# A spectral mixer on one core: column 0 of the filtered blocks given to GpSimd, with a new order of the middle stage

## The chip, the cores and the metric

The kernel runs on one core of one Trainium2 chip. The core has a matrix engine (TensorE, in the profile PE, with its weight loads as PEld), a vector engine (VectorE, DVE), an activation engine (ScalarE, ACT), a general engine (GpSimd, POOL) and an engine that here only issues transfers (SyncE, SP). Each engine runs its own queue of instructions in order; queues wait for each other through semaphores. The metric is the device time of one execution in microseconds, as the median of several runs.

## The reference

For `x` of 2048 tokens by 512 channels:

```python
xn = layernorm(x)                                  # over the 512 channels
s  = irfft2(rfft2(xn) * (w_r + 1j * w_i))          # a filter in two dimensions
u  = gelu(einsum("bsd,sf->bdf", xn, w1) + b1)      # mixes the tokens, f = 1792
y  = einsum("bdf,fs->bds", u, w2) + b2
out = x + s * silu(transpose(y))
```

All inputs and outputs are float32. The two matrix products of the mixer are the bulk of the work. A float32 operand is kept as a large part (the value rounded to what TensorE multiplies at speed) and a small part (the remainder), and a product is made of three products of parts: large by large, large by small, small by large.

## The kernel before

The tokens are cut into 16 tiles `j` of 128 tokens. The program has three stages, followed by a short tail of stores.

*First stage* (0 to 98 us): for each tile the layernorm's moments on VectorE, the normalised tile as large and small part (`hh`, `hl`), the products with seven of the fourteen blocks of `w1` (`hidden_early`, L396), and the first transform of the tile for the filter (`first_transform`, L226), whose result VectorE and GpSimd fold into the array `ey`. Ahead of the first product, TensorE runs `WARM` products of zeros (L385) from the tile `wz`, which GpSimd sets to zero (L373). `hidden_early` issues the large and then the small part of the weight against `hh`, calls `between`, which is the transform of this tile, and then multiplies by `hl`. The statistics of a tile are made by `stats` (L185), `spreads` (L189 to L195) and `scales` (L199 to L206).

*Middle stage* (98 to 204 us): the products with the other seven blocks of `w1` (the stream `h`, with `L683`, `L684` for the large weight part, `L686`, `L692` for the small one, `w1l`), between which the filter is worked off. The filter comes in four groups `n` with two halves `h` each. For each (n, h): TensorE transforms along the channels and forward (L591, L605); ScalarE takes the result from the accumulator into a block `e` (`taken`); two transfers on SyncE's queue make `z`, a copy of `e` with neighbouring rows swapped (`swapped`); VectorE works out the filtered block `pq` from `e`, `z` and the weights `wa`, `wb` in ten instructions (`weighted`); and TensorE transforms `pq` back (`way_back`, L670), 64 small products for both halves of `n`.

The column 0 of a block holds signals whose weights differ from the other columns (a real transform packs two real values there). GpSimd works it out apart in three instructions on 128x4 elements (`columns_apart`, the stream `s`): `z` times `e1`, `e` times `e2`, and their sum into the small tile `s1`; VectorE's copy then sets it over column 0 of `pq`. VectorE's instructions that write `e` must wait until GpSimd has read column 0 of it. Two rows of group 0 are special too: VectorE clears them in `z`, and GpSimd and VectorE combine the weights of these rows in `load_weights` and `ends_too`.

The order of all engines' work in the middle stage is written out by hand. Each letter of `STEPS` takes the next instruction from a stream: `h` products, `u` the filter's TensorE units, `r` raw weight loads, `a` large parts on ScalarE, `o` small parts on VectorE, `d` small parts by an accumulating transfer on GpSimd's queue (w1l 18, 20, to 28: ScalarE writes the negative of the large part, the transfer adds the raw weight), `g` gelu, `i`, `b` copies on ScalarE, `e` taken, `x` swapped, `s` GpSimd's column 0, `w` weighted, `l`, `t` loads of filter weights and tables, `f`, `q`, `m` forms of `u` for the second product (ScalarE's large parts, VectorE's small parts, VectorE's four sums). As each engine works in order, this list sets what stands behind what on every queue. `pq` has one buffer for each half `h`, so a block's first write waits for the `way_back` of the group before.

*Third stage* (204 to 375 us): eight passes `p` of products with `w2` (L961 to L967), whose parts ScalarE and VectorE make (L781, L782), the filter's last two transforms for the two tiles `p` and `p + 8` (L876, L885), the gates (L916) and `finish` (L926 to L931): it multiplies by the gate and stores. Tiles below 15 are stored by an accumulating transfer on GpSimd's queue onto `out`, into which `x` was copied earlier; tile 15 has `x` added on VectorE and is stored by SyncE.

## Time and profile before

| | |
|---|---|
| median of 3 runs | 379.05 us (379.03 to 380.07) |
| profiled execution | 381.97 us, span 380.2 us, granted clock 1.00 |
| TensorE busy | 369.4 us, 97% of the span |
| VectorE busy | 328.9 us, 87% |
| ScalarE busy | 213.8 us, 56% |
| GpSimd busy | 104.1 us, 27% |
| middle stage, 98 to 204 us | TensorE 104.2, VectorE 99.9, ScalarE 62.5, GpSimd 45.9 us busy |

In the profile a row of a timeline has the start, the duration, the engine, the source line, the operation, output and inputs by the program's names, and behind them in brackets how long the engine was idle before and what ended that. A row of groups ends with busy time and mean duration in ns, and behind the last bar the idle time before these instructions and its releasers. L128 is the line of the helper that issues the middle stage's instructions. A row of waits has an engine, what it worked on, whom it waited for, the total in us, the number of times and the longest.

### The profile page before, as it was taken

Reading aid. Unit: us, or ns where it says so; the run is one execution under the profiler, and the core shown is the slowest. Engines: PE = TensorE matmul, PEld = TensorE weight load, DVE = VectorE, ACT = ScalarE, POOL = GpSimd, SP = SyncE. Lnnn points to the kernel's source line nnn. Section 1 sums busy time; section 2 is a strip of 40 time slices with the busy share of each in tenths; the row PEclk is TensorE's granted clock in tenths of the full one; section 3 lists DMA queues with packets and bytes.
Section 4 is the critical chain, followed back from the end, with each engine's and each line's share of the span. In section 5 each row is a group of like instructions: output and inputs, shape, how many; then the busy total and the mean of one; then the engine's idle time right before and its main releaser. Section 6 shows DMA issues by size and latency. Waiting matters only on the chain.

```text
span 380.2 us, 6865 instructions
## 1 busy us (share of the span) xinstructions
PE 369.4 (97%) x2417; PEld 311.8 (82%) x2417; DVE 328.9 (87%) x717; ACT 213.8 (56%) x391; POOL 104.1 (27%) x134
## 2 busy tenths in 40 slices
PE   8999999999999999999999999999999999999994
PEld 4888888888778676778688787798988888888994
DVE  6899999867799999999978895998888988898873
ACT  4677765754973365855466753564555455545641
POOL 2133233243420835856300021030302021110100
PEclk9999999999999999999999999999999999999999
DMA  7957468214546777999863898989989889895711
GB/s 252 344 166 225 151 203 256 81 42 140 145 160 201 240 230 267 260 279 314 182 177 52 234 249 184 269 161 265 192 222 198 204 212 183 229 195 180 99 22 41
DMA packets 42087, 73.28 MB, mean 193 GB/s; under 512 B 4196, under 2 KB 25444, under 8 KB 41924
## 3 DMA queue, kind: packets, MB, share of 16 engines
q1 hardware_dynamic: 35460, 58.88, 49.3%
q0 software_dynamic: 6592, 13.96, 22.2%
q8 instruction: 19, 0.31, 0.3%
q14 instruction: 16, 0.13, 0.1%
HBM read 60.24 MB, written 8.13 MB: 180 GB/s over the span
## 4 chain that ended last, share of the span: by engine, by line
PE 83%; DVE 9%; DMA 3%; issue 2%; ACT 2%; POOL 0%; DVEq 0%; ACTq 0%; POOLq 0%
PE ps L396 20%; PE ps L961 16%; PE ps L963 8%; PE ps L683 6%; PE ps L684 5%; PE ps L967 5%; PE ps L591 4%; PE ps L226 4%; PE ps L692 4%; PE ps L885 3%; PE ps L876 3%; DMA s<-in_w_dram 3%; DVE pq L128 2%; DVE e L128 2%; PE ps L670 1%
## 5 line engine op out<-in xcount | busy, mean ns | idle before, releaser
L396 PE MATMUL ps<-h,w1h 128*128 128x512 f32 x224 | 58.7, 398 | 0.0
L781 ACT ACTIVATE w2f<-s 128x896 fp32r<-128x896 f32 x32 | 30.2, 947 | 32.4 <-DVE s L808 16.9
L396 PEld LDWEIGHTS ps<-h,w1h 128*128 128x128 f32 x224 | 40.9, 188 | 7.9
L772 POOL DMA_DIRECT2D s<-in_w_dram x16 | 13.8, 864 | 118.1 <-DVE es L890 31.4
L782 DVE TENSOR_TENSOR w2f<-s,w2f 128x896 fp32r<-128x896 f32 x32 | 34.8, 1089 | 11.9 <-ACT w2f L781 11.3
L683 PE MATMUL ps<-h,w1h 128*128 128x512 f32 x112 | 45.0, 401 | 0.0
L684 PE MATMUL ps<-h,w1h 128*128 128x512 f32 x112 | 43.7, 390 | 0.0
L128 POOL TENSOR_TENSOR s<-z,e 128x4 f32<-128x4 f32 x8 | 27.4, 3429 | 37.3 <-DMA z<-e 25.2
L961 PE MATMUL ps<-fa,w2f 128*128 128x512 f32 x98 | 36.3, 406 | 0.4 <-DVE p L909 0.4
L961 PE MATMUL ps<-fc,w2f 128*128 128x512 f32 x98 | 35.2, 397 | 1.4 <-DVE p L909 0.9
L961 PE MATMUL ps<-fb,w2f 128*128 128x512 f32 x98 | 35.8, 402 | 0.0
L782 DVE TENSOR_TENSOR w2f<-a,w2f 128x896 fp32r<-128x896 f32 x24 | 26.1, 1087 | 6.1 <-ACT w2f L781 6.1
L396 PE MATMUL ps<-h,w1l 128*128 128x512 f32 x112 | 30.6, 389 | 0.0
L781 ACT ACTIVATE w2f<-a 128x896 fp32r<-128x896 f32 x24 | 22.6, 948 | 13.6 <-PE ps L963 9.3
L128 ACT ACTIVATE w1h<-w1s 128x512 fp32r<-128x512 f32 (+1 forms) x30 | 17.5, 582 | 22.6 <-PE ps L684 13.0
L683 PEld LDWEIGHTS ps<-h,w1h 128*128 128x128 f32 x112 | 21.0, 188 | 9.2 <-issue 5.0
L963 PE MATMUL ps<-fc,w2f 128*128 128x256 f32 x98 | 27.7, 283 | 0.4 <-DVE w2f L782 0.4
L963 PE MATMUL ps<-fa,w2f 128*128 128x256 f32 x98 | 27.7, 282 | 0.1
L963 PE MATMUL ps<-fb,w2f 128*128 128x256 f32 x98 | 27.6, 282 | 0.0
L928 POOL DMA_DIRECT2D out_dram<-g x16 | 14.2, 887 | 44.6 <-DVE g L926 44.6
L692 PE MATMUL ps<-h,w1l 128*128 128x512 f32 x93 | 25.6, 391 | 0.1
L396 PEld LDWEIGHTS ps<-h,w1l 128*128 128x128 f32 x112 | 21.0, 188 | 4.6
(179 smaller groups left out, 918.4 us busy)
## 6 DMA issues: line engine op xcount, KB each, us to landing
a<-in_w_dram SPq DMA_DIRECT2D x24, 448.0 KB
s<-in_w_dram POOLq DMA_DIRECT2D x17, 448.0 KB, 7.5
s<-in_w_dram SPq DMA_DIRECT2D x15, 448.0 KB
w1r<-in_w_dram SPq DMA_DIRECT2D x16, 256.0 KB
z<-e SPq DMA_DIRECT2D x16, 256.0 KB
w1s<-in_w_dram SPq DMA_DIRECT2D x16, 256.0 KB
yj<-ey SPq DMA_DIRECT2D x16, 256.0 KB
x<-in_x_dram SPq DMA_DIRECT2D x15, 256.0 KB
```

The lines of the kernel that those rows point to most:

```text
L128: return lambda *a, **k: keep(getattr(engine, name)(*a, **k))
L226: T.matmul(z[:, b], h[:, b * P:(b + 1) * P], c, start=True, stop=True)
L396: T.matmul(ps[:, bank + i], w[wi][:, i * P:(i + 1) * P], hj, start=first and j == 0, stop=last and j == NJ - 1)
L591: keep(T.matmul(pd[:, b * P:(b + 1) * P], ey[:, lo, b].rearrange("p h j -> p (h j)"), cd[:, b], start=True, stop=True))
L683: keep(T.matmul(o, wh[:, sl], hh[j], start=first, stop=False))
L684: keep(T.matmul(o, wh[:, sl], hl[j], start=False, stop=False))
L692: keep(T.matmul(ps[:, bank], wl[:, k * P:k * P + P], hh[j], start=False, stop=final))
L781: ordered(A.activation(wf[:, 0], v, AF.Copy))
L782: ordered(V.tensor_sub(wf[:, 1], v, wf[:, 0].bitcast(F32)))
L961: in_turn(j0, T.matmul(o, wf[:, 0, i], u, start=m == 0 and not joins, stop=end, skip_group_check=True))
L963: in_turn(j0, T.matmul(o[:, HD:], wf[:, 1, i], u[:, :HD], start=False, stop=end, skip_group_check=True))
L967: T.matmul(o, wf[:, wi, i], ui, start=m + a == 0 and opens, stop=end and a == 2, skip_group_check=joins)
```

## The change

- `WARM` goes from 16 to 12, and `wz` is a tile of 128 columns that the warm-up products read four times.
- In the first tile, `normed_v` comes before the shift `nb` (new function `shifts`); the small part of the first weight is made before the second tile's moments, and the second tile's `spreads` and `scales` come later. The transform of tile 0 comes behind its products with `hl`.
- Column 0 is GpSimd's from end to end: `columns_apart` writes the sum into column 0 of `pq` itself, `weighted` works on the columns from 1 on, and VectorE's copy is gone. The clearing of the special rows of `z` and the combination of their weights go to GpSimd.
- `STEPS` is another list.
- In `finish`, the right half of tile 7 has `x` added on VectorE (loaded as `x0`) and is stored by SyncE, as tile 15's halves are.

```diff
@@ -21,15 +21,15 @@
 NH = NF // 2
 FORMS = (2, 1, 0, 3, 4, 5, 6)
 NS = 25
-WARM = 16
+WARM = 12
 LATE = 16
 ADDED = range(NJ + 2, 2 * NJ - 2, 2)
 STEPS = (
-    "aahoguogogurigurfifrqufqirqhfmhiqmumahmfthoeerhfxmuxqaxmuxiomruqifmuiqhfwswhisswhgfwsfsuwsahwehwwhwl"
...
+    "orauaroghorghiugrguiffqufqihqfmiqhamumhoftmhreefxumaxqxuioxmruqimugmihfhswsihsfqfswfusqahswhshowrweh"
...
 )
 SPLIT = 4
 
@@ -195,12 +195,16 @@
                 keep(V.bn_aggr(m["mv"][:, i], m["st"][:, i]))
             roots(m)
 
-        def scales(m):
+        def shifts(m):
+            keep(V.scalar_tensor_tensor(m["nb"], m["mv"][:, :, 0:1], -1.0, m["rs"][:, :, 1:2], op0=ALU.mult, op1=ALU.mult))
+
+        def scales(m, alone=False):
             keep(V.reciprocal(m["r0"], m["sd"]))
             keep(V.tensor_mul(m["t"], m["r0"], m["r0"]))
             keep(V.scalar_tensor_tensor(m["t"], m["t"], -0.5, m["v2"], op0=ALU.mult, op1=ALU.mult))
             keep(V.scalar_tensor_tensor(m["rs"], m["t"], 1.5, m["r0"], op0=ALU.add, op1=ALU.mult))
-            keep(V.scalar_tensor_tensor(m["nb"], m["mv"][:, :, 0:1], -1.0, m["rs"][:, :, 1:2], op0=ALU.mult, op1=ALU.mult))
+            if not alone:
+                shifts(m)
 
             G.tensor_mul(m["q"], m["rs"][:, :, 0:1], m["rs"][:, :, 1:2])
             G.tensor_mul(m["q"], m["q"], m["v2"][:, :, 1:2])
@@ -369,7 +373,7 @@
             return t[:, k]
 
 
-        wz = lnp.tile([P, D], BF16, name="wz", tag="e")
+        wz = lnp.tile([P, P], BF16, name="wz", tag="e")
         G.memset(wz, 0.0)
         WA, WB = (0, 4, w1p, 4), (NH, 3, wbp, 3)
         xs[0] = lnp.tile([P, D], F32, name="x0", tag="x", bufs=5)
@@ -382,7 +386,7 @@
         SY.dma_start(cf, c_f)
         load_x(2)
         for _ in range(WARM):
-            T.matmul(ps[:, 0], wz[:, :P], wz, start=True, stop=True)
+            T.matmul(ps[:, 0].rearrange("p (b c) -> p b c", c=P), wz, wz.unsqueeze(1).to_broadcast([P, 4, P]), start=True, stop=True)
 
         def high(dst, src):
             keep(A.activation(dst, src, AF.Copy))
@@ -396,9 +400,9 @@
                     T.matmul(ps[:, bank + i], w[wi][:, i * P:(i + 1) * P], hj, start=first and j == 0, stop=last and j == NJ - 1)
             products(0, hh[j], True, False)
             products(1, hh[j], False, False)
-            r = between()
+            r = between() if j else None
             products(0, hl[j], False, True)
-            return r
+            return r or between()
 
         m = moments("m0", 2)
         for i, c_ in enumerate(halves):
@@ -409,18 +413,19 @@
         w = w1_tiles(0, *WA), w1_tiles(0, *WB)
         h = new_h(0)
         high(w[0][0], raws[0, 0])
-        scales(m)
+        scales(m, alone=True)
         normed_v(hh[0], xs[0], m, 0, 1)
+        shifts(m)
         normed(h, xs[0], m, 0)
         m1 = moments("m1", 1)
+        low(w[0][1], raws[0, 0], w[0][0])
         stats(m1, 0, xs[1])
-        low(w[0][1], raws[0, 0], w[0][0])
-        spreads(m1, 1)
         high(w[1][0], raws[0, 1])
         c = turned(0, m, 0)
         low(hl[0], h, hh[0])
+        spreads(m1, 1)
+        low(w[1][1], raws[0, 1], w[1][0])
         scales(m1)
-        low(w[1][1], raws[0, 1], w[1][0])
         of = {1: (m1, 0)}
         m = moments("m2", 2)
         of.update({2: (m, 0), 3: (m, 1)})
@@ -543,12 +548,10 @@
                 SY.dma_start(w[:2, 0], wx[:, 0:3:2])
                 SY.dma_start(w[2:], wk[2:, at:at + 2, i::2])
                 SY.dma_start(w[:2, 1], wk[:2, at + 1, i::2])
-                G.tensor_sub(w[:2, 0, 1 - i], w[:2, 0, 1 - i], w[:2, 0, i])
-
-        def ends_too(k, i):
-            if k == ends // 2:
-                one, two = (weights[k, i][:2, 0, a] for a in (1 - i, i))
-                V.scalar_tensor_tensor(two, two, 2.0, one, op0=ALU.mult, op1=ALU.add)
+                one, two = (w[:2, 0, a] for a in (1 - i, i))
+                G.tensor_sub(one, one, two)
+                G.tensor_add(two, two, two)
+                G.tensor_add(two, two, one)
 
         def place(n, h):
             places[n, h] = [mp.tile([P, 2, 2, 256], F32, name=f"{c}{n}_{h}", tag=f"ez{h}", bufs=2) for c in "ez"]
@@ -576,7 +579,7 @@
         G.tensor_copy(e2[:2, ends, 1:2], e1[:2, ends, 1:2])
         G.tensor_scalar(e1, e1, sg[:, 0:1], None, op0=ALU.mult)
 
-        hfs, s1s, back = {}, {}, {n: [] for n in range(4)}
+        hfs, back = {}, {n: [] for n in range(4)}
 
         def load_tables(n):
             if n not in gfs:
@@ -619,23 +622,30 @@
             yield SY.dma_start(z[0::2], e[1::2])
             yield SY.dma_start(z[1::2], e[0::2])
 
+        def products_of(n, h):
+
+            k = 2 * n + h
+            if k not in pqs:
+                pqs[k] = new_pq(n, h)
+            return pqs[k]
+
         def columns_apart(n, h):
 
             at, (e, z) = 4 * n + 2 * h, places[n, h]
-            s1 = s1s[n, h] = mp.tile([P, 2, 2, 2], F32, name=f"s1_{n}_{h}", tag="s1")
+            if at == ends:
+                yield G.memset(z[:2, 0], 0.0)
+            s1 = mp.tile([P, 2, 2, 2], F32, name=f"s1_{n}_{h}", tag="s1")
             yield G.tensor_mul(s1[:, 0], z[:, :, :, 0], e1[:, at:at + 2])
             yield G.tensor_mul(s1[:, 1], e[:, :, :, 0], e2[:, at:at + 2])
-            yield G.tensor_add(s1[:, 0], s1[:, 0], s1[:, 1])
+            yield G.tensor_add(products_of(n, h)[:, :, :, 0], s1[:, 0], s1[:, 1])
 
         def weighted(n):
 
             for h in range(2):
                 at, k = 4 * n + 2 * h, 2 * n + h
                 e, z = places[n, h]
-                if at == ends:
-                    yield V.memset(z[:2, 0], 0.0)
-                pq = pqs.pop(k, None) or new_pq(n, h)
-                er, ei, zr, zi, pr, pi = (a[:, :, s] for a in (e, z, pq) for s in range(2))
+                pq = products_of(n, h)
+                er, ei, zr, zi, pr, pi = (a[:, :, s, 1:] for a in (e, z, pq) for s in range(2))
                 V.scalar_tensor_tensor(pr, zi, sg[:, 0:1], er, op0=ALU.mult, op1=ALU.add)
                 yield
                 V.scalar_tensor_tensor(pi, zr, sg[:, 0:1], ei, op0=ALU.mult, op1=ALU.subtract)
@@ -644,12 +654,9 @@
                 yield
                 V.scalar_tensor_tensor(ei, zr, sg[:, 1:2], ei, op0=ALU.mult, op1=ALU.subtract)
                 yield
-                for i in range(2) if k == ends // 2 else ():
-                    yield ends_too(k, i)
-                V.tensor_mul(pq, pq, weights[k, 0])
-                yield
-                V.tensor_mul(e, e, weights[k, 1])
-                yield
+                for a, i in ((pq, 0), (e, 1)):
+                    V.tensor_mul(a[..., 1:], a[..., 1:], weights[k, i][..., 1:])
+                    yield
                 V.tensor_add(pr, pr, pi)
                 yield
                 V.tensor_add(er, er, ei)
@@ -657,8 +664,6 @@
                 V.tensor_sub(pi, pr, er)
                 yield
                 V.tensor_add(pr, pr, er)
-                yield
-                V.tensor_copy(pq[:, :, :, 0], s1s[n, h][:, 0])
                 back[n].append(pq)
                 yield
 
@@ -924,7 +929,7 @@
 
         def finish(g, j, cols, y, xr=None):
             V.tensor_mul(g[:, cols], y[:, cols], g[:, cols])
-            if j + 1 < NJ:
+            if xr is None:
                 G.dma_start(out[:, j, cols], g[:, cols], accum_op=ALU.add)
             else:
                 V.tensor_add(g[:, cols], g[:, cols], xr[:, cols])
@@ -942,6 +947,8 @@
             if p == NP - 1:
                 xr = fp.tile([P, D], F32, name="xr", tag="yj", bufs=3)
                 SY.dma_start(xr, x[:, NJ - 1])
+                x0 = w2p.tile([P, NH * P], F32, name="x0", tag="s1", bufs=1)[:, :D]
+                SY.dma_start(x0[:, right_], x[:, j0, right_])
             both = p + 1 < NP
             bx, by, bz, bw = (ps[:, b] if both else ps[:, b, :HD] for b in (2 + p % 2, 4, 5, 1))
             for k, n in enumerate(ORDER if p + 1 < NP else LAST):
@@ -985,7 +992,7 @@
                 elif n == 3:
                     gate(g0, j0, right_, summed(f"c12_{p}", bz, v2), 1.0)
                     if p:
-                        finish(g0, j0, whole if p + 1 < NP else right_, y0)
+                        finish(g0, j0, *((whole, y0) if p + 1 < NP else (right_, y0, x0)))
                     else:
                         y0 = channels(j0, yt0)
                         yt1 = sequence(j1, yb)
```

Line numbers after the change are 4 higher in the first stage and 5 higher from the middle stage on (L670 becomes L675, L692 becomes L697, L926 becomes L931).

VectorE's queue at the end of block (0,1), where its second half of the filter's first group is finished, before:

```order
L128 TENSOR_TENSOR pq0_1_1326<-pq0_1_1326,e0_1_1324 128x2x256 [waits DVE_49]
L128 TENSOR_TENSOR w1l_11_1645<-w1s11_1593,w1h_11_1644 128x384 [waits DMAHW4_49,DMAHW5_49,PE_49,Activation_49]
L128 COPY pq0_1_1326<-s1_0_1_1515 128x4 [waits DVE_49,Pool_49]
L128 TENSOR_TENSOR w1l_12_1666<-w1s12_1608,w1h_12_1665 128x384 [waits DMAHW0_49,DMAHW1_49,PE_49,Activation_49]
L128 TENSOR_TENSOR fb1_1481<-u1_1294,fb1_1481 128x2x256
L128 TENSOR_TENSOR fd0_1511<-u0_1358,fd0_1511 128x256
L128 TENSOR_TENSOR fa0_1512<-u0_1358,fa0_1512 128x2x256
```

and in the change:

```order
L128 TENSOR_TENSOR pq0_1_1326<-pq0_1_1326,e0_1_1324 128x2x255 [waits DVE_49]
L128 TENSOR_TENSOR w1l_11_1637<-w1s11_1582,w1h_11_1636 128x384 [waits DMAHW4_49,DMAHW5_49,PE_49,Activation_49]
L128 TENSOR_TENSOR w1l_12_1660<-w1s12_1595,w1h_12_1659 128x384 [waits DMAHW6_49,DMAHW7_49,PE_49,Activation_49]
L128 TENSOR_TENSOR fa0_1510<-u0_1374,fa0_1510 128x2x256
L128 SCALAR_TENSOR_TENSOR pq1_0_1718<-z1_0_1556,sg_1304,e1_0_1555 128x2x255 [waits DMAHW0_49,DMAHW1_49,PE_49,Pool_49]
```

The copy is gone, and the form subtractions `fb1` and `fd0`, which stood here, now stand ahead of block (0,1).

GpSimd's queue for the blocks (3,0) and (3,1), before:

```order
L128 TENSOR_TENSOR s1_3_0_2117<-s1_3_0_2117 128x4 [waits Pool_49]
L128 DMA w1l_24_2177<-in_w1_dram 128x2x256 [waits DMASW2_49,DMASW0_49,Activation_49]
L128 TENSOR_TENSOR s1_3_1_2228<-z3_1_2083,e1_69 128x4 [waits DMAHW3_49,DMAHW2_49,DVE_49]
L128 TENSOR_TENSOR s1_3_1_2228<-e3_1_2082,e2_70 128x4
L128 TENSOR_TENSOR s1_3_1_2228<-s1_3_1_2228 128x4 [waits Pool_49]
L128 DMA w1l_26_2235<-in_w1_dram 128x2x256 [waits DMASW3_49,DMASW1_49,Activation_49]
```

and in the change:

```order
L128 TENSOR_TENSOR pq3_0_2167<-s1_3_0_2103 128x4 [waits DVE_49,PE_49,Pool_49]
L128 DMA w1l_24_2176<-in_w1_dram 128x2x256 [waits DMASW2_49,DMASW0_49,Activation_49]
L128 TENSOR_TENSOR s1_3_1_2211<-z3_1_2065,e1_69 128x4 [waits DMAHW2_49,DMAHW1_49]
L128 TENSOR_TENSOR s1_3_1_2211<-e3_1_2064,e2_70 128x4
L128 TENSOR_TENSOR pq3_1_2224<-s1_3_1_2211 128x4 [waits DVE_49,Pool_49]
L128 DMA w1l_26_2231<-in_w1_dram 128x2x256 [waits DMASW3_49,DMASW1_49,Activation_49]
```

The sums now write `pq`, and that of (3,0) waits for TensorE, which must have read the `pq` of the group before; the transfers of `w1l` still stand behind them.

TensorE's queue at `way_back(3)`, before:

```order
L684 MATMUL ps_58<-h10_97,w1h_26_2234 128x512
L692 MATMUL ps_58<-h10_97,w1l_26_2235 128x512 [waits DMASW3_49,Activation_49]
L692 MATMUL ps_58<-h10_97,w1l_26_2235 128x512 x3
L670 MATMUL ps_58<-pq3_0_2188,hf3_1955 32x256 [waits DMAHW5_49,DVE_49]
L670 MATMUL ps_58<-pq3_0_2188,hf3_1955 32x256 x7
L670 MATMUL ps_58<-pq3_1_2265,hf3_1955 32x256 [waits DVE_49]
```

and in the change:

```order
L675 MATMUL ps_58<-pq3_0_2167,hf3_1949 32x256 [waits DMAHW5_49,DVE_49,Pool_49]
L675 MATMUL ps_58<-pq3_0_2167,hf3_1949 32x256 x7
L675 MATMUL ps_58<-pq3_1_2224,hf3_1949 32x256 [waits DVE_49,Pool_49]
L675 MATMUL ps_58<-pq3_1_2224,hf3_1949 32x256 x7
L675 MATMUL ps_58<-pq3_0_2167,hf3_1949 32x256 x8
L675 MATMUL ps_58<-pq3_1_2224,hf3_1949 32x256 x8
L688 MATMUL ps_58<-h10_97,w1h_26_2230 128x512
L689 MATMUL ps_58<-h10_97,w1h_26_2230 128x512
L697 MATMUL ps_58<-h10_97,w1l_26_2231 128x512 [waits DMASW3_49,Activation_49]
```

`way_back(3)` stands ahead of the second half of part 26 instead of behind it, and waits for GpSimd too.

8 lines of the change are left out of this document (4 added, 4 removed).

## The prediction

> **What bounds the kernel now.** I read the page's busy shares first, then the waits of TensorE, then the three places at which the change works: the start, the middle stage from 98 to 204 us, and the last few microseconds.
>
> ```profile
> PE 369.4 (97%) x2417; PEld 311.8 (82%) x2417; DVE 328.9 (87%) x717; ACT 213.8 (56%) x391; POOL 104.1 (27%) x134
> ...
> 98.00:204.00 106.00, 104.18 (x848) 81.02 (x848) 99.91 (x166) 62.48 (x109) 45.94 (x38) 1.00 0.77 222
> ...
> PE ps L670 <- DVE pq L128: 1.2, 2, 0.7
> PE ps L686 <- DVE w1l L128: 0.5, 1, 0.5
> ```
>
> TensorE is busy for 369.4 of 380.2 us, at a granted clock of 1.00 in the middle stage (second row: the stage, its length, then the busy time of TensorE's products, its weight loads, VectorE, ScalarE and GpSimd, with instruction counts), and no product is removed that the reference needs. So the change can win only what TensorE does not spend on products: its waits, the start before the first product and the end behind the last. In the middle stage VectorE is busy 99.91 of 106 us, nearly as full as TensorE (104.18), and it is VectorE that TensorE waits for there: for the filtered block `pq` and for the small part `w1l` of a weight. A microsecond taken off VectorE is worth something only up to these waits. The profiled execution took 381.97 us, its span of 380.2 and 1.8 around it; the median of the runs, 379.05 us, is 2.9 lower. I work out differences inside the profiled span, where what lies around it stays, and take them off the median.
>
> **The end: -0.7 us.**
>
> ```profile
> 374.47 0.86 POOL L928 DMA_DIRECT2D out_dram<-g  x1 [9.58 <-DVE g L926]
> 375.14 0.47 ACT L916 ACTIVATE g<-ps,b2t 128x256 f32<-128x256 f32 x1 [1.42 <-PE ps L967]
> 375.65 0.43 DVE L926 TENSOR_TENSOR g<-y,g 128x256 f32<-128x256 f32 x1 [1.47 <-ACT g L916]
> 376.11 0.42 DVE L930 TENSOR_TENSOR g<-g,xr 128x256 f32<-128x256 f32 x1
> ...
> L1042 POOLq DRAIN  x3: 46/93/4971, 374.4 to 379.9; - x3
> L1042 SPq DRAIN  x3: 7/7/7, 378.6 to 379.7; - x3
> ```
>
> GpSimd issues its last store at 374.47, and its drain, which begins there, takes 4.97 us: to 379.4. SyncE, which sends the really last result after 376.5, is through at 378.7. So GpSimd's drain is the last to arrive, by 0.7 us. The change makes that store a plain one on SyncE, with the addition of `x0` on VectorE; the drain then starts after GpSimd's store before it, some 9.6 us earlier by the idle time in the first row. The added 128x256 addition (0.42, as L930's) falls into the 1.47 us that VectorE idles before 375.65; without that cover it would cost its 0.42. The `x0` load, 128 KB more on SyncE's queue, has the whole last pass to land. Range 0 to -0.8.
>
> **The start: -0.2 us.**
>
> ```profile
> 0.75 0.52 POOL L373 MEMSET wz<- 128x512 bf16 x1
> 1.33 5.38 PE L385 MATMUL ps<-wz 128*128 128x512 bf16 x16 [1.33 <-POOL wz L373]
> 5.04 1.18 PEld L385 LDWEIGHTS <-wz 128*128 128x128 bf16 x6 [0.16 <-issue]
> ...
> 5.26 0.63 ACT L388 ACTIVATE w1h<-w1r 128x512 fp32r<-128x512 f32 x1 [0.78 <-DMA w1r<-in_w_dram]
> 5.37 0.54 DVE L212 TENSOR_SCALAR h<-x,mvm,rsm 128x512 fp32r<-128x512 f32 x1
> 6.36 1.27 PE L396 MATMUL ps<-h,w1h 128*128 128x512 f32 x4
> ```
>
> The operands of the first product are there at 5.37 + 0.54 = 5.91 and 5.26 + 0.63 = 5.89, but the sixteen warm-up products hold TensorE until 6.36. Their last six follow each other every 0.2 us (1.18 for six), so without four of them the warm-up ends 0.8 us earlier, at about 5.5, earlier still as the memset fills a quarter of the columns; the first product can come at 5.9, 0.45 earlier. Against it, the second tile's small statistics now stand behind one more subtraction of some 0.6 us on VectorE, and later tiles do not come 0.45 us earlier; I take 0.2. With the warm-up over before the products begin, a gap of some 0.4 us opens on TensorE; the trace has none of that kind to price, so it is bounded by nothing and by the whole gain. Range 0 to -0.6.
>
> [...]
>
> **The middle: -1.8 us.** Here VectorE loses work:
>
> ```profile
> L128 DVE COPY pq<-s 128x4 f32<-128x4 f32 x8 | 1.3, 163 | 0.1
> L128 DVE MEMSET z<- 2x512 f32 x1 | 0.5, 485 | 0.0
> L128 DVE SCALAR_TENSOR_TENSOR wa<-wa 2x256 f32<-2x256 f32 x1 | 0.4, 406 | 0.0
> L128 DVE SCALAR_TENSOR_TENSOR e<-z,sg,e 128x512 f32<-128x512 f32 x16 | 11.3, 745 | 0.3 <-POOL s L128 0.3
> ...
> L128 POOL TENSOR_TENSOR wb<-wb 2x256 f32<-2x256 f32 x1 | 0.8, 776 | 0.0
> ```
>
> Eight copies at 0.08 start to start (129.89 to 129.97 below) are 0.65; memset 0.5; the special-row instruction 0.41, less the 0.08 by which neighbours overlap, and its like for `wb`, 0.67; the waits for GpSimd's reading of column 0 0.3: together 2.1 us. Blocks of 255 columns in place of 256 save 0.4%, which I leave out. GpSimd gets the memset and four additions of 0.78 next to the one shown, 3 us, ahead of its 12.1 us of idleness before block (0,0) (the idle time in the row of its first products, under rival 1).
>
> ```profile
> 128.77 0.66 PE L670 MATMUL ps<-pq,hf 32*32 32x256 f32 x16
> 128.82 0.67 DVE L128 TENSOR_TENSOR pq<-pq,e 128x512 f32<-128x512 f32 x1
> 129.43 0.54 DVE L128 TENSOR_TENSOR w1l<-w1s,w1h 128x384 fp32r<-128x384 f32 x1
> 129.89 0.15 DVE L128 COPY pq<-s 128x4 f32<-128x4 f32 x1
> 129.97 0.54 DVE L128 TENSOR_TENSOR w1l<-w1s,w1h 128x384 fp32r<-128x384 f32 x1
> 130.10 1.36 PE L670 MATMUL ps<-pq,hf 32*32 32x256 f32 x48 [0.67 <-DVE pq L128]
> ...
> 147.14 0.54 DVE L128 TENSOR_TENSOR w1l<-w1s,w1h 128x384 fp32r<-128x384 f32 x1
> 150.00 1.60 PE L670 MATMUL ps<-pq,hf 32*32 32x256 f32 x64
> ...
> 187.82 0.66 PE L670 MATMUL ps<-pq,hf 32*32 32x256 f32 x16
> 188.98 1.36 PE L670 MATMUL ps<-pq,hf 32*32 32x256 f32 x48 [0.50 <-DVE pq L128]
> ```
>
> `way_back(1)` has its blocks in time and takes 1.60. `way_back(0)` takes 128.77 to 131.46, 1.1 too long, and `way_back(3)` 187.82 to 190.34, 0.9 too long; with 0.5 for `w1l` these are the 2.5 us to be had. (0) Ahead of block (0,1) VectorE loses memset, special rows, one copy and 0.1 of waits, 1.4 us, and takes on two form subtractions that stood behind it (0.6 start to start for 128x512, as from 128.82 to 129.43, and 0.33 for half of it): it is 0.45 earlier. Its last addition ends at 129.05, and TensorE no longer waits for the `w1l` and the copy behind it but goes on at about 129.1 in place of 130.10: 1.0 won. (1) At 147.14 VectorE is then 1.8 earlier (1.4, the rest of the waits, two copies) and TensorE 1.0: the 0.5 goes, 1.5 in all. (3) `way_back(3)` now stands 1.4 us earlier in TensorE's order, half a part of products, and VectorE's block comes 2.1 earlier; so TensorE, 1.5 earlier, still loses about 0.6 of the 0.9. Sum 1.0 + 0.5 + 0.3 = 1.8. The third stage is fed by loads whose room `way_back(3)` frees, so what is won there is not given back to the loads. Bounds: nothing where other waits take the place, -2.5 where all go.
>
> Sum: -0.7 - 0.2 - 1.8 = -2.7, **376.4 us**. The middle's 1.8 stands on GpSimd being in time: `way_back` on TensorE, with all products behind it, now waits for GpSimd's addition into `pq`, that addition waits for the `way_back` before, and the `w1l` transfers of GpSimd's queue stand behind it.
>
> **Rival 1, slower: GpSimd is locked out.**
>
> ```profile
> L128 POOL TENSOR_TENSOR s<-z,e 128x4 f32<-128x4 f32 x8 | 27.4, 3429 | 37.3 <-DMA z<-e 25.2 <-DVE z L128 12.1
> ...
> 124.96 8.47 POOL L128 TENSOR_TENSOR s<-z,e 128x4 f32<-128x4 f32 x1 [10.16 <-DMA z<-e]
> 133.39 0.20 POOL L128 TENSOR_TENSOR s<-e,e 128x4 f32<-128x4 f32 x1
> 135.53 0.72 POOL L128 TENSOR_TENSOR s<-z,e 128x4 f32<-128x4 f32 x1 [1.67 <-DMA z<-e]
> 175.81 4.15 POOL L128 TENSOR_TENSOR s<-z,e 128x4 f32<-128x4 f32 x1 [3.49 <-DMA z<-e]
> 181.29 1.20 POOL L128 DMA_DIRECT2D w1l<-in_w_dram  x1
> ...
> w1l<-in_w_dram POOLq DMA_DIRECT2D x6, 256.0 KB, 6.0
> ...
> 133.62 1.45 DVE L128 SCALAR_TENSOR_TENSOR e<-z,sg,e 128x512 f32<-128x512 f32 x2 [0.25 <-POOL s L128]
> 179.82 0.17 DVE L128 COPY pq<-s 128x4 f32<-128x4 f32 x1
> ```
>
> A product of 128x4 that takes 0.20 us undisturbed took 8.47 and 4.15. The long ones end where VectorE, busy until then with two-input instructions, idles for GpSimd (133.43, before 133.62) or runs a copy (179.96); the one at 135.53 got in at the next boundary, 0.72. The change takes away just these openings. The place is block (3,1): if its first product, ready at about 174, misses the boundaries, VectorE next pauses between dependent `u` subtractions behind the block, whose last addition I put 2.1 and some before `way_back(3)`'s 188.98: at about 185.6. Behind it 1.3 us (179.96 to 181.29) and 6.0 of transfer: `w1l` lands at about 193, where TensorE wants it behind `way_back(3)`, at 188.98 + 1.36 - 2.9 = 187.4. Cost 5.5, less the 2.7: 381.8. It decides from an entry later than about 180 (187.4 - 6.0 - 1.3) on. For it speaks the mean of 3.43 us of eight first products; against it, that some got in at once, and that VectorE will also pause for `w1l` buffers that TensorE still reads.
>
> [...]
>
> **Rival 2, no change: it costs only block (1,0).** If that one (ready at about 124.5) is held until the dependent `u` instructions (six instructions behind the `w1l` of 147.14, which comes at 145.3: at about 148), the six instructions of (1,0) and (1,1) follow at some 0.4 each; `way_back(1)`, due at 150.00 - 1.5 - 0.5 = 148.0 (it stands half a microsecond of products earlier too), waits 2.5 us: nearly all of the 2.7 is gone, 379.0. For it: 8.47 us at just this block.
>
> **Rival 3: only the ends pay.** Another wait takes the place of those in the middle, as ScalarE's for the buffers of blocks that GpSimd still reads. Then -0.9: 378.1.
>
> **How the numbers follow.** Forecast 0.50, rival 1 0.25, rival 2 0.15, rival 3 0.10. A difference within 0.3% (1.1 us) cannot be told from none. Faster: 0.50 and half of rival 3, 0.55; same: the rest of it and rival 2, 0.20; slower 0.25. The forecast's own range is 375.2 (all terms at the far bound: 3.9 off) to 377.9; the whole range, 375.0 to 381.9, takes in rivals 2 and 3 and half of rival 1, 0.85 in all.
>
> **What would show it.** Right: no idle before L675 for `way_back(0)` over 0.5, none for `w1l` by VectorE at 146, GpSimd's first products under 3 us or ended by 180, first product at 5.9, SyncE last at the end. Wrong: TensorE's waits name POOL or a `w1l` transfer at L675 or L697; a first product of `s` over 10 us; first products at L400 at twice their 0.2 us pace.

## The result: 376.38 us, a ratio of 0.992

The kernel with the change takes 376.38 us (median of 6 runs, 376.13 to 378.69), the kernel before beside it 379.32 (6 runs, 379.03 to 380.07). The ratio is 0.9918, with a 95% interval of 0.990 to 0.9937: faster, by more than the 0.3% that can be told from no change. On another chip a second comparison gave 0.9932 (0.9899 to 0.9965). The profiled execution took 378.69 us, its span 376.9, the granted clock 1.00. The ratios of this document leave out executions in which the chip was in a slower state, so they can differ by some 0.1% from the quotient of the medians beside them.

The page's row of busy times, and the windows view of the middle stage (its length, then busy time of TensorE's products, its weight loads, VectorE, ScalarE and GpSimd), of the changed kernel:

```profile
PE 368.5 (98%) x2413; PEld 311.1 (83%) x2413; DVE 326.8 (87%) x707; ACT 213.5 (57%) x391; POOL 107.4 (28%) x138
...
97.90:201.80 103.90, 103.48 (x849) 80.86 (x848) 97.29 (x154) 62.10 (x109) 50.45 (x44) 1.00 0.78 226
```

VectorE lost 2.6 us of work in the middle stage (97.29 for 99.91 before; 0.4 of it is one instruction on `u` that no longer falls into the stage), and the stage is 2.2 us shorter (103.9 for 106.1). TensorE is still what the stage is full of.

TensorE's waits in the changed kernel (L968 was L961 before: from the last pass's two new lines on, line numbers are 7 higher):

```profile
PE ps L890 <- ACT yt L883: 1.2, 1, 1.2
PE ps L389 <- POOL wz L377: 1.0, 1, 1.0
PE ps L968 <- DVE fc L300: 0.5, 1, 0.5
...
PE ps L675 <- DVE pq L128: 0.4, 2, 0.2
```

The wait for `w1l` is gone from this list, that for the filtered block `pq` has fallen from 1.2 to 0.4, and a new one, for `yt`, stands in the third stage; "start alone" below, with the old middle stage, has it too (0.6).

TensorE's timeline at the places of the prediction:

```profile
128.40 0.66 PE L675 MATMUL ps<-pq,hf 32*32 32x256 f32 x16
129.25 1.35 PE L675 MATMUL ps<-pq,hf 32*32 32x256 f32 x48 [0.19 <-DVE pq L128]
...
147.86 1.50 PE L675 MATMUL ps<-pq,hf 32*32 32x256 f32 x64
...
184.61 0.66 PE L675 MATMUL ps<-pq,hf 32*32 32x256 f32 x16
185.45 1.35 PE L675 MATMUL ps<-pq,hf 32*32 32x256 f32 x48 [0.18 <-DVE pq L128]
...
187.30 1.09 PE L697 MATMUL ps<-h,w1l 128*128 128x512 f32 x4
```

`way_back(0)` now takes 128.40 to 130.60, 2.2 us for 2.7 before, and `way_back(3)` 184.61 to 186.80, 2.2 for 2.5. An undisturbed one takes 1.50, as `way_back(1)` at 147.86.

Where the span went is best seen stage by stage. The table gives the start of the first product, the end of the first stage's last product, and from there the time to the first `w2f` product (middle), to the end of the last product (third), and to the end of the span, worked out from the start and end times of TensorE's rows in each trace. The experiments are explained below.

| kernel | first product | first stage ends | middle | third | behind last product |
|---|---|---|---|---|---|
| before | 6.36 | 97.91 | 106.1 | 171.1 | 5.1 |
| start alone | 5.95 | 97.72 | 106.2 | 168.9 | 5.1 |
| end alone | 7.07 | 98.43 | 106.1 | 168.0 | 4.2 |
| list alone | 6.89 | 98.25 | 106.5 | 168.1 | 5.0 |
| code alone | 6.17 | 97.97 | 103.2 | 173.8 | 5.2 |
| code and list | 6.98 | 98.34 | 103.8 | 168.0 | 5.1 |
| code and end | 7.43 | 98.79 | 103.2 | 171.0 | 4.2 |
| full change | 6.16 | 97.92 | 103.9 | 170.9 | 4.2 |
| full change, again | 6.04 | 97.80 | 103.9 | 169.1 | 4.2 |

Between the two profiled executions, then: start 0.0, middle -2.2, third stage -0.2, end -0.9, together -3.3. The columns "middle" and "behind last product" fall into two groups each, whatever else varies; the third stage varies between the traces by up to 5.7 us, with old and new code alike (see the last section). So the terms of the sum can be read stage by stage where the whole times scatter too much.

### The profile page after: what moved, and what is told of

It is laid out like the page before. It is cut to its first block, busy times and chain, and to the rows that moved or that the text cites. A ratio compares the mean times of both kernels' runs of the same rounds, so it can differ in the third digit from the quotient of the medians.

```text
span 376.9 us, 6860 instructions
## 1 busy us (share of the span) xinstructions
PE 368.5 (98%) x2413; PEld 311.1 (83%) x2413; DVE 326.8 (87%) x707; ACT 213.5 (57%) x391; POOL 107.4 (28%) x138
## 3 DMA queue, kind: packets, MB, share of 16 engines
HBM read 60.38 MB, written 8.13 MB: 182 GB/s over the span
## 4 chain that ended last, share of the span: by engine, by line
PE 78%; DVE 10%; DMA 6%; ACT 3%; issue 2%; SPq 0%; DVEq 0%; ACTq 0%
PE ps L400 18%; PE ps L968 15%; PE ps L970 8%; PE ps L688 6%; PE ps L689 6%; PE ps L974 5%; PE ps L697 4%; PE ps L594 4%; PE ps L230 3%; DMA a<-in_w_dram 3%; PE ps L890 3%; PE ps L881 3%; DMA s<-in_w_dram 2%; DVE pq L128 2%; PE ps L675 1%
## 5 line engine op out<-in xcount | busy, mean ns | idle before, releaser
L400 PEld LDWEIGHTS ps<-h,w1h 128*128 128x128 f32 x224 | 40.8, 188 | 9.0 <-ACT w1h L392 1.2
L786 ACT ACTIVATE w2f<-s 128x896 fp32r<-128x896 f32 x32 | 30.2, 947 | 29.9 <-DVE s L813 16.9
L968 PE MATMUL ps<-fa,w2f 128*128 128x512 f32 x98 | 36.3, 406 | 0.4 <-DVE p L914 0.4
L968 PE MATMUL ps<-fb,w2f 128*128 128x512 f32 x98 | 35.8, 402 | 0.0
L968 PE MATMUL ps<-fc,w2f 128*128 128x512 f32 x98 | 35.1, 397 | 0.5 <-DVE fc L300 0.5
L688 PEld LDWEIGHTS ps<-h,w1h 128*128 128x128 f32 x112 | 21.0, 188 | 8.9 <-issue 5.0
L697 PE MATMUL ps<-h,w1l 128*128 128x512 f32 x93 | 25.7, 391 | 0.0
L689 PEld LDWEIGHTS ps<-h,w1h 128*128 128x128 f32 x112 | 21.1, 188 | 3.9
```

Source lines behind the costliest of these rows:

```text
L400: T.matmul(ps[:, bank + i], w[wi][:, i * P:(i + 1) * P], hj, start=first and j == 0, stop=last and j == NJ - 1)
L688: keep(T.matmul(o, wh[:, sl], hh[j], start=first, stop=False))
L689: keep(T.matmul(o, wh[:, sl], hl[j], start=False, stop=False))
L697: keep(T.matmul(ps[:, bank], wl[:, k * P:k * P + P], hh[j], start=False, stop=final))
L786: ordered(A.activation(wf[:, 0], v, AF.Copy))
L968: in_turn(j0, T.matmul(o, wf[:, 0, i], u, start=m == 0 and not joins, stop=end, skip_group_check=True))
```

## The experiments

**The pieces one by one.** The first four runs put the change's pieces into the kernel before. "End alone" adds only the plain store:

```diff
-            if j + 1 < NJ:
+            if xr is None:
                 G.dma_start(out[:, j, cols], g[:, cols], accum_op=ALU.add)
...
+                x0 = w2p.tile([P, NH * P], F32, name="x0", tag="s1", bufs=1)[:, :D]
+                SY.dma_start(x0[:, right_], x[:, j0, right_])
```

> The kernel before with the plain store of tile 7's right half alone. Theory: GpSimd's drain is the last to arrive at the end, and the store moved to SyncE takes it off: 0.7 to 0.95 us less than before, all of it behind the last product. Rival: the end is bound by SyncE's own last store and its landing; then nothing, or 0.4 more by the addition on VectorE.

Measured: 379.05 beside 379.77, a ratio of 0.9993 (0.9961 to 1.0024). The times cannot tell 0.7 from nothing here. The traces can: 4.2 us behind the last product in this and in every other kernel that has the plain store, 5.0 to 5.2 in every one without. The end is worth 0.9.

"Start alone" is the full change with the middle and the end taken back: `WARM = 12`, the memset of a quarter of the columns, and the first tiles' small steps in their new order.

```diff
-WARM = 16
+WARM = 12
...
-        scales(m)
+        scales(m, alone=True)
         normed_v(hh[0], xs[0], m, 0, 1)
+        shifts(m)
```

> The kernel before with the change's start alone (12 warm-up products, the new order of the first tile). Theory after the two profiles: no gain, within 0.15 us of before, because the first product comes 0.2 us earlier but tile 2's transform starts where it did (19.95 before, 19.94 after). Rival, as predicted: 0.2 us less.

Measured: 379.79, ratio 1.0005 (0.9979 to 1.0032): no gain in the time that this comparison could show, though an interval of 1 us to either side does not exclude a few tenths.

"Code and list" is the columns' code on GpSimd with the new list `STEPS`, with the old start and end. Its diff is the middle part of the change, of which this is the core:

```diff
-    "aahoguogogurigurfifrqufqirqhfmhiqmumahmfthoeerhfxmuxqaxmuxiomruqifmuiqhfwswhisswhgfwsfsuwsahwehwwhwl"
+    "orauaroghorghiugrguiffqufqihqfmiqhamumhoftmhreefxumaxqxuioxmruqimugmihfhswsihsfqfswfusqahswhshowrweh"
...
-            yield G.tensor_add(s1[:, 0], s1[:, 0], s1[:, 1])
+            yield G.tensor_add(products_of(n, h)[:, :, :, 0], s1[:, 0], s1[:, 1])
...
```

> The kernel before with column 0 on GpSimd and the new list, with before's start and end. Theory: the third stage begins 2.1 us earlier than before, and the time is 1.9 to 2.3 us less. Rival: part of the gain came from the start; then 1.7 to 1.9 less.

Measured: 377.92, ratio 0.9952 (0.9922 to 0.9981). "Code alone" has the same code with the list of before; the list's letters change only where the code has fewer or more steps, and three of GpSimd's additions are moved behind the `way_back` whose buffer they need:

```diff
-            yield G.tensor_add(s1[:, 0], s1[:, 0], s1[:, 1])
+            yield G.tensor_add(products_of(n, h)[:, :, :, 0], s1[:, 0], s1[:, 1])
...
-                yield
-                V.tensor_copy(pq[:, :, :, 0], s1s[n, h][:, 0])
```

> Column 0 on GpSimd, but before's list (its letters for the removed instructions taken out, GpSimd's sums of blocks (1,0), (2,0), (3,0) put right behind the way_back whose buffer they need); before's start and end. Theory: VectorE's 2.1 us less is what counts, way_back(0) loses its wait of about 1 us and the w1l wait at 147.7 goes: 1.3 to 1.9 us less than before. Rival: it is the list that brings the gain, and the code alone brings 0 to 0.7, or costs, as GpSimd's sums come late for TensorE.

Measured: 376.81, ratio 0.9911 (0.9875 to 0.9946). "List alone" is the kernel before with the new list, and nothing else (the letters of steps that the old code has more of are put in):

```diff
-    "aahoguogogurigurfifrqufqirqhfmhiqmumahmfthoeerhfxmuxqaxmuxiomruqifmuiqhfwswhisswhgfwsfsuwsahwehwwhwl"
+    "orauaroghorghiugrguiffqufqihqfmiqhamumhoftmhreefxumaxqxuioxmruqimugmihfhwwsihsfqfswfusqahswhshowrwww"
...
```

> Before's code with the new list (letters for VectorE's memset, special rows and eight copies put in at their places); before's start and end. Theory: the list alone moves way_back(3) and two forms, but VectorE has its 2.1 us back: 0 to 0.6 us less than before. Rival: the list brings most, 1.2 us or more.

Measured: 379.71, ratio 1.0004 (0.9981 to 1.0027). So it is the code that wins in the middle, and the list made anew wins nothing. The table says more: beside the old code the new list makes the middle 0.4 longer (106.5 for 106.1), beside the new code 0.7 (103.8 in "code and list", 103.9 in the full change, for 103.2). Which part of the code wins it (the copies, the special rows, or the shorter blocks of 255 columns) was not run apart. The list alone, waits of TensorE and its timeline at `way_back(0)` and `way_back(3)`:

```profile
PE ps L670 <- DVE pq L128: 1.6, 2, 1.2
...
PE ps L692 <- DVE w1l L128: 1.2, 1, 1.2
```

```profile
129.82 0.66 PE L670 MATMUL ps<-pq,hf 32*32 32x256 f32 x16
130.88 1.36 PE L670 MATMUL ps<-pq,hf 32*32 32x256 f32 x48 [0.40 <-DVE pq L128]
...
188.34 1.36 PE L670 MATMUL ps<-pq,hf 32*32 32x256 f32 x48 [1.24 <-DVE pq L128]
```

The waits for VectorE are no smaller than before, only at other places. With the new code and the old list they are gone, as the next kernel shows.

**Code and end.** The code with the old list, the plain store, and the old start: the pieces that won something.

```diff
...
-            if j + 1 < NJ:
+            if xr is None:
                 G.dma_start(out[:, j, cols], g[:, cols], accum_op=ALU.add)
...
+                x0 = w2p.tile([P, NH * P], F32, name="x0", tag="s1", bufs=1)[:, :D]
+                SY.dma_start(x0[:, right_], x[:, j0, right_])
```

> The columns' code on GpSimd with the old list, and the plain store at the end, with the old start. Theory (list and start bring nothing, code and end all): 0.4 to 0.9 us below the run with the code alone, so about 376.0, a ratio to before of 0.989 to 0.991, no slower than the full change. Rival (the new list or the short warm-up earn a part that shows only beside the code): slower than the full change by 0.5 us or more.

Measured: 376.64, ratio 0.9928 (0.9898 to 0.9959); the full change beside it, on the same chip and expected as follows, took 376.55.

> The full change once more, to stand on the same chip as the others of this batch: a ratio to before of 0.992, as in the first comparison.

Ratio 0.9932 (0.9899 to 0.9965). The two cannot be told apart in time, so the rival (a part that only the list or the short warm-up earns) finds no support, and no version here beats the full change by a measurable amount. The trace shows where "code and end" is better and where worse. Its timeline of TensorE at `way_back(0)` and `way_back(3)`:

```profile
129.24 1.50 PE L670 MATMUL ps<-pq,hf 32*32 32x256 f32 x64
...
186.39 1.92 PE L670 MATMUL ps<-pq,hf 32*32 32x256 f32 x64
```

`way_back(0)` runs through in 1.50. VectorE, in the same kernel, does two subtractions of forms only behind block (0,1):

```profile
128.04 0.69 DVE L128 TENSOR_TENSOR pq<-pq,e 128x510 f32<-128x510 f32 x1
128.64 1.02 DVE L128 TENSOR_TENSOR w1l<-w1s,w1h 128x384 fp32r<-128x384 f32 x2
129.58 0.68 DVE L128 TENSOR_TENSOR fb<-u,fb 128x512 fp32r<-128x512 f32 x1
130.18 0.42 DVE L128 TENSOR_TENSOR fd<-u,fd 128x256 fp32r<-128x256 f32 x1
```

The block's last addition ends at 128.73, 29.9 us after the first stage's end; in the full change, at 129.11, it is 31.2 after it. Of these 1.3 us the two subtractions that the new list puts ahead of the block are 0.9 (129.58 to 130.52 in these rows). What "code and end" wins there it gave up at the start of this execution, whose first product came at 7.43. The code and the end with the short warm-up and the old list, which should take the better of each, was not run.

**The small steps of the second tile.** In my comparison the first product came 0.20 earlier and the first stage ended no earlier. A kernel with the change's twelve warm-up products and the old order of the first tiles' small steps was to show whether those steps eat the gain:

```diff
-        scales(m, alone=True)
+        scales(m)
         normed_v(hh[0], xs[0], m, 0, 1)
-        shifts(m)
         normed(h, xs[0], m, 0)
```

> The full change, but with the old order of the first tile's small steps, and 12 warm-up products as in the full change. Theory (the 0.2 us won by the short warm-up is lost where the second tile's small steps come 0.5 later): the second tile's step on ScalarE starts at 9.1 instead of 9.6 us and the first stage ends 0.1 to 0.3 us earlier than in the full change. Rival (the first stage's end is set by something later than these steps): it ends at the same time, 97.9.

Measured: 377.21, ratio 0.9932 (0.9901 to 0.9963). The step on ScalarE came at 9.08, as expected, and the first stage ended at 97.97, not earlier than the 97.92 and 97.80 of the full change. The theory falls. This stage ends between 97.7 and 98.0 in all eight traces with the short warm-up. The time is lost early: from the start of the 61st product on, at 18.4 to 18.6 in these traces and 18.6 to 19.5 in those of the long warm-up, all of them take the same 79.3 to 79.4 us to the stage's end. In the full change a product at 18.0 starts 0.26 behind its pace, released by ScalarE's `w1h`, and the next one 0.11; in the kernel of this section neither does, but its second product of all starts 0.34 behind its pace. Why the two orders come out alike is not shown.

**GpSimd's sum made late.** The prediction let rival 1 decide from an entry later than 180 us on. The changed kernel sent the `w1l` transfer at 178.38, with 4.3 us to spare between its landing and its use. Two kernels delay the addition into `pq` of block (3,1) by memsets on GpSimd, 13 or 26 of them:

```diff
             yield G.tensor_mul(s1[:, 1], e[:, :, :, 0], e2[:, at:at + 2])
+            if (n, h) == (3, 1):
+                idle = mp.tile([P, 192], F32, name="idle", bufs=1)
+                for _ in range(13):
+                    G.memset(idle, 0.0)
```

> The changed kernel with 13 memsets of a scratch tile (about 4 us) on GpSimd between the second product and the sum of block (3,1): GpSimd comes late by a known time. Theory: w1l 26 landed at 182.98 and was wanted at 187.30, so 4 us cost less than 0.5 us: 376.2 to 377.0. Rival 1 as predicted puts the limit near an entry at 180, which leaves 3 us from 177: then some 1 us, 377.4.

> The same with 26 memsets (about 8 us). Theory: the transfer of w1l 26 lands 8 us later, 3.7 us after TensorE wants it: 379.5 to 380.5, with a TensorE wait for a transfer at L697 (or its line in this kernel) of 2.5 to 3.5 us. Rival: the wait is at way_back(3) for GpSimd's sum instead, about 1 us, and the transfer is hidden: 377.5.

Measured: 385.33 with 13 (ratio 1.0134, 1.0083 to 1.0184), and 384.29 with 26 (1.0114, 1.0076 to 1.0152). Both expectations were wrong. The first, which still saw a gain over the kernel before, counted the delay and not that a late addition also finds its door shut (the door: a moment at which VectorE's program lets a GpSimd instruction in); the second had the right wait, though 2.5 to 3.5 us long, and left out the one at `way_back(3)` and what the clock adds. GpSimd's timeline with 13 memsets:

```profile
177.71 4.06 POOL L128 MEMSET idle<- 128x192 f32 x13
181.73 4.56 POOL L128 TENSOR_TENSOR pq<-s 128x4 f32<-128x4 f32 x1
186.23 2.44 POOL L128 DMA_DIRECT2D w1l<-in_w_dram  x2
```

The addition stood ready at 181.73 and was held to 186.29, until VectorE's dependent `u` instructions, so the transfer went out 7.9 us late for a delay of 4.06. With 26 memsets (8.17 us) the addition came at 186.05, took 0.45 and let the transfer go at 186.44: here the delay itself reaches to the open door. So half the delay brings the same lateness, and with 13 it is the door that sets it. TensorE's waits with 13 memsets, and the windows view (its granted clock is the third number from the end):

```profile
PE ps L701 <- DMA w1l<-in_w_dram: 6.1, 1, 6.1
PE ps L679 <- POOL pq L128: 1.1, 1, 1.1
```

```profile
191.00:194.00 3.00, 0.00 (x0) 0.00 (x0) 0.00 (x0) 1.13 (x3) 0.00 (x0) 0.73 1.12 291
194.00:197.00 3.00, 2.48 (x6) 2.03 (x7) 0.34 (x1) 0.00 (x0) 0.00 (x0) 0.50 0.42 157
197.00:200.00 3.00, 3.00 (x10) 2.33 (x9) 2.49 (x5) 0.27 (x1) 1.74 (x2) 0.63 0.14 18
200.00:203.00 3.00, 3.00 (x15) 2.47 (x14) 2.19 (x5) 0.67 (x2) 0.00 (x1) 1.00 0.95 162
```

The middle stage takes 113.4 us, 9.5 more than in the full change. Of this 7.2 are the two waits; behind the long one TensorE runs at a granted clock of 0.50 and 0.63, 6 products in 2.5 us and 10 in 3 us where later 15 go into 3. With 26 the waits are 4.4 and 1.1, and the stage is 8.1 longer.

**What opens the door.** In the changed kernel four of GpSimd's six long waits ended at the first of the four instructions by which VectorE begins a block, and these read a scalar per partition, `sg`. This kernel puts constants in its place (1 and -1; the filter's signs are left out, all the rest is done):

```diff
-                V.scalar_tensor_tensor(pr, zi, sg[:, 0:1], er, op0=ALU.mult, op1=ALU.add)
+                V.scalar_tensor_tensor(pr, zi, 1.0, er, op0=ALU.mult, op1=ALU.add)
...
-                V.scalar_tensor_tensor(ei, zr, sg[:, 1:2], ei, op0=ALU.mult, op1=ALU.subtract)
+                V.scalar_tensor_tensor(ei, zr, -1.0, ei, op0=ALU.mult, op1=ALU.subtract)
```

> The changed kernel with the constants 1 and -1 in place of the two per-partition sign columns in VectorE's four first instructions of each block, so the filter's signs are left out and the output is not the reference's. In the profile after, four of GpSimd's six long products end just before the next block's first such instruction. Theory: the instruction that reads a per-partition scalar lets GpSimd in; without it GpSimd stays out until a pause (from 124.7 to about 148 for block (1,0)), way_back(1) waits 2 us or more, 378 us or more. Rival: it is the place (a block's first instruction with its waits for transfers, TensorE and GpSimd) that lets it in; then the products end where they did and the time is 376.4 within 0.5.

Measured: 385.94, ratio 1.0159 (1.0113 to 1.0206): 9.6 us above the 376.38 of the full change, by four constants in each block; 8.0 of it is in the middle stage. GpSimd's timeline and TensorE's waits:

```profile
110.40 0.69 POOL L128 TENSOR_TENSOR s<-z,e 128x4 f32<-128x4 f32 x1
...
124.45 19.45 POOL L128 TENSOR_TENSOR s<-z,e 128x4 f32<-128x4 f32 x1 [10.48 <-DMA z<-e]
...
174.47 12.14 POOL L128 TENSOR_TENSOR s<-z,e 128x4 f32<-128x4 f32 x1 [1.18 <-DMA z<-e]
```

```profile
PE ps L697 <- DMA w1l<-in_w_dram: 4.5, 1, 4.5
PE ps L675 <- POOL pq L128: 1.3, 1, 1.3
```

The product of block (1,0) was held for 19.45 us, over two blocks' first instructions, until VectorE stood idle for ScalarE (143.86 to 145.41); that of (3,1) for 12.14, to the `u` pair at 186.6. For block (3,1) this is rival 1 as it was drawn: block, door and transfer. But the constant does not always shut GpSimd out: the six instructions of the blocks (0,0) and (0,1) got in at once (0.40 to 0.69 us each, the first row), between VectorE's instructions with the constant and others that followed without a pause.

The last kernel adds to this one a copy of 128x4 ahead of each block's first instruction, to test whether any instruction of another kind opens the door (signs left out as before):

```diff
+                spare = mp.tile([P, 2, 2, 4], F32, name=f"spare{k}", tag="spare", bufs=1)
+                V.tensor_copy(spare[:, :, :, 0], e1[:, 0:2])
                 V.scalar_tensor_tensor(pr, zi, 1.0, er, op0=ALU.mult, op1=ALU.add)
```

> The kernel with constants in place of the per-partition signs (the filter's signs left out), and a one-input copy of 128x4 ahead of the first such instruction of each block. Theory (an instruction of VectorE that isn't of the two-tensor kind lets GpSimd in): the 19.4 us product ends at the next block's start, at about 6 us, w1l comes in time, and the time is 377 instead of 386. Rival (GpSimd needs idle time of VectorE, and the per-partition scalar is a coincidence): the 19.4 us product stays and the time is 386.

Measured: five executions, 376.36, 376.67 and 378.01, and 386.98 and 389.54; the trace is of the one of 386.98. Neither expectation holds for all five. GpSimd's timeline, and VectorE's at the two block starts in it:

```profile
124.26 5.99 POOL L128 TENSOR_TENSOR s<-z,e 128x4 f32<-128x4 f32 x1 [10.16 <-DMA z<-e]
130.21 8.12 POOL L128 TENSOR_TENSOR s<-e,e 128x4 f32<-128x4 f32 x1
138.41 8.13 POOL L128 TENSOR_TENSOR pq<-s 128x4 f32<-128x4 f32 x1
```

```profile
130.11 0.17 DVE L128 COPY spare<-e 128x4 f32<-128x4 f32 x1
130.18 1.28 DVE L128 SCALAR_TENSOR_TENSOR pq<-z,e 128x510 f32<-128x510 f32 x2
...
138.18 0.17 DVE L128 COPY spare<-e 128x4 f32<-128x4 f32 x1
```

The copy at 130.11 let in one instruction of GpSimd, and the next waited a whole block, 8.12 us, for the copy at 138.18; the third waited 8.13 us until VectorE idled. So these copies were a door, but one with room for one, and GpSimd has three instructions a block; in the full change the four instructions with the scalar let all three in, one behind the other (0.70 and 0.58 in the rows of the next section). In (3,1) the second product came too late and the addition was held to 187.00; TensorE then waited 5.9 us for `w1l` and 1.1 for `pq`, much as with the 13 memsets, and that fits the 387. That the three short executions had these in time is only argued: no trace of one was taken.

## Why the prediction was right, step by step

The time (376.4 predicted, 376.38 measured), the sign and the likeliest case came out. The agreement is partly luck: the terms are each off by a few tenths, and the sum was taken off a median of 379.05, where the kernel before took 379.32 in the comparison. The change brought 2.9 there, and 3.3 between the two profiled spans, for the 2.7 predicted.

**The end: -0.7 predicted, -0.9 measured.** The changed kernel's last result on VectorE, its stores on SyncE, and the drains:

```profile
370.52 4.02 SPq L936 DMA_DIRECT2D out_dram<-g  x3
...
373.75 0.42 DVE L935 TENSOR_TENSOR g<-g,xr 128x256 f32<-128x256 f32 x1
```

```profile
L1049 POOLq DRAIN  x3: 46/93/4967, 361.7 to 376.7; - x3
L1049 SPq DRAIN  x3: 7/7/7, 376.1 to 376.4; - x3
```

GpSimd's drain, as long as before (4.97), now begins at 361.7 and is over 10 us before the end. SyncE is last. The mechanism is as drawn; the size was short by 0.2, and is beyond my far bound of 0.8. I had compared GpSimd's drain with SyncE's drain at 378.7, but that one moved too: from 2.2 us behind VectorE's last result (376.53) to 1.9 (374.17).

**The start: -0.2 predicted, 0.0 between the two profiles, -0.4 on the mean of all traces.** The changed kernel, start of TensorE's timeline:

```profile
1.02 5.05 PE L389 MATMUL ps<-wz 128*128 128x512 bf16 x12 [1.02 <-POOL wz L377]
6.16 1.17 PE L400 MATMUL ps<-h,w1h 128*128 128x512 f32 x4
```

and that of "end alone", which starts as before:

```profile
1.33 6.08 PE L385 MATMUL ps<-wz 128*128 128x512 bf16 x16 [1.33 <-POOL wz L373]
7.07 1.28 PE L396 MATMUL ps<-h,w1h 128*128 128x512 f32 x4
```

The step that failed is the warm-up's own duration. I took the 5.38 us of one profile for its length. Sixteen products took 5.38 in that execution, 6.08 in this one and 6.44 in "code and end", so over six traces the first product came between 6.17 and 7.43; with twelve it came between 5.95 and 6.21 in eight. My expected end of the warm-up at 5.5 was wrong too (it was 6.07), and the first product came at 6.16, not 5.9. The products that ran from 5 to 7 us scatter with it, 10 in the kernel before, 7 in "end alone" and 6 in "code and end", though the granted clock reads 1.00 in all three; why the same warm-up takes a different time from execution to execution was not shown. The first stage ended at 98.28 on the mean of the six (97.91 to 98.79) and at 97.88 on that of the eight: -0.4, inside the range of 0 to -0.6, a term that the profile of the kernel before, the earliest of the six, happened not to show.

**The middle: -1.8 predicted, -2.2 measured**, inside the range of 0 to -2.5. `w1l`: the 0.5 is gone, as predicted. `way_back(3)`: 0.3 won and the rest still lost, as predicted. `way_back(0)`: 1.0 predicted, 0.5 measured (2.69 to 2.20 long); the other 0.7 of what it loses remains, since VectorE's block comes behind the two subtractions that the new list puts ahead of it. I had counted those two, but let TensorE go on at 129.1; it went on at 129.25, and its part began 0.4 earlier than I had it. The rest of the 2.2 is in small pieces that I had not counted as waits; `way_back(1)`, for one, is 0.10 shorter (1.60 to 1.50). What the prediction missed altogether is that the list has a price: with the old list the same code makes the middle 2.9 shorter, beyond the bound that I set, and no `way_back` of (0) to (2) waits. That the row with "0.67 <-DVE pq" could go wholly I had seen only as a bound.

**Rival 1 (GpSimd locked out: 381.8).** It did not come, and not for the reason that I gave against it. GpSimd's timeline in the changed kernel, at block (3,1), and VectorE's at the same time:

```profile
173.54 3.58 POOL L128 TENSOR_TENSOR s<-z,e 128x4 f32<-128x4 f32 x1 [0.80 <-DMA z<-e]
177.08 0.70 POOL L128 TENSOR_TENSOR s<-e,e 128x4 f32<-128x4 f32 x1
177.86 0.58 POOL L128 TENSOR_TENSOR pq<-s 128x4 f32<-128x4 f32 x1
178.38 1.20 POOL L128 DMA_DIRECT2D w1l<-in_w_dram  x1
```

```profile
176.38 0.68 DVE L128 TENSOR_TENSOR pq<-pq,e 128x510 f32<-128x510 f32 x1
176.98 1.40 DVE L128 SCALAR_TENSOR_TENSOR pq<-z,sg,e 128x510 f32<-128x510 f32 x2
178.30 1.40 DVE L128 SCALAR_TENSOR_TENSOR e<-z,sg,e 128x510 f32<-128x510 f32 x2
```

The product is held as before and gets in exactly where the row of instructions with `sg` begins; the next two follow at its boundaries. Four of the six long ones end there, one at the `u` pair, one in an idle 0.35. The premise "the change takes away just these openings" was false: the doors of before (the copies, the idle) were not the only ones. The trace of before shows this one too: its product at 179.92 took 0.77, beside the two instructions with `sg` that begin at 179.90. In the kernel with constants GpSimd stayed out for 19.45 us, longer than any single VectorE instruction of the block (1.21 us at most), so a boundary between two of them was not enough by itself. What decides at a boundary whether GpSimd gets in was not shown.

The rival's price was of the right kind and too small. Where the constants bring it about, the waits are 1.3 and 4.5, 5.8 in all for the 5.5 that I wrote; but the middle is 8.0 longer than in the full change (112.0 for 103.9), and most of the 2.2 beyond the waits is TensorE's return at half clock (0.52 granted from 194 to 197 us, 8 products where 15 go into 3 us). That term was missing.

**Rivals 2 and 3.** (1,0) was held for 5.98 us, but its sum was there long before `way_back(1)`, which ran in 1.50 at 147.86; even at 19.45 us (the kernel with constants) that one was not late. So the hold to 148 that I drew does not come about: in that kernel VectorE idles for ScalarE at 144. That only the ends pay is refuted by "code alone", which has none of the ends and a ratio of 0.9911.

**The signs.** Right: no wait for `w1l`, 0.19 before `way_back(0)`, the last first product of GpSimd ended at 177.1, SyncE last. Wrong: the first product at 5.9.

## What to carry to other kernels

Small work given to GpSimd beside a busy VectorE was worth here what VectorE was waited for and little more (the code alone made the middle 2.9 us shorter, for a bound of 2.5 from the waits), and it was safe only as long as VectorE's program had places at which GpSimd got in (with the constants it was held for 12.14 us at block (3,1), and the whole took 9.6 longer): look for the rows at which its long instructions end, count how many it needs per block, and see that the last of them comes before the transfer or the product that waits behind. A late instruction missed its door and was later by a whole stretch of VectorE's program (7.9 us for a delay of 4.06), and TensorE's waits, the longest of each kernel 4.4 to 6.1 us, cost a third to a half as much again, most of it in clock (7.2 us of waits cost 9.5, 5.8 cost 8.0, 5.5 cost 8.1). Time a reordered list by itself beside the change that it came with: here the code won 2.9 us in the middle and the list gave 0.7 back.
